# Fused retention attention and adapter mixture: short units stored in 64-row transfers, loads requested earlier, the fourth unit's scores moved, the last unit's slots in banks of their own

## The chip, the cores and the metric

The kernel runs on one core of one Trainium2 chip. The metric is device time in microseconds (us), the median over several executions. A core has a matrix engine (PE in the profile, with PEld for its weight loads), a vector engine (DVE), a scalar engine (ACT), a general engine (POOL) and a sync engine (SP); each runs its own instructions in order, and they meet through semaphores. DMA transfers are issued by SP, ACT or POOL and are carried by 16 DMA engines. Matrix results land in PSUM, which has eight banks that the kernel names by number.

## The reference

```python
scores = scale * q @ k^T                       # per batch (8) and head (8), 576 positions, 64 wide
Dmat   = where(i >= j, gamma_h ** (i - j), 0)  # decay mask
ret    = (scores * Dmat) @ v
x      = ret as rows (8 * 576 = 4608) x (8 heads * 64 = 512)
logits = x @ w_gate                            # 8 experts
top two experts per row, weights = softmax over the two
delta  = sum over the two of weight * ((x @ A[e]) @ B[e])     # rank 16
out    = x + delta                             # float32, 4608 x 512
```

## The kernel before, in words

The 576 positions of a sequence are four chunks of 128 and a last one of 64. A *unit* is one chunk of two batches; the last chunk takes four batches in one unit, with two batches on partitions 0 to 63 and two on 64 to 127 (a *short* unit). There are 18 units, t = 0 to 17; units 16 and 17 are short. A *quad* is one chunk of four batches, that is two full units or one short one, and `load(n, which)` fetches q, k or v of quad n: 1 MB for a full quad (4096 pieces of 256 B), and for a short one two transfers of 64 partitions. Each of q, k and v has three buffers, so quad n can be loaded when quad n-3 has been used up.

Per unit, with the function that issues each step: `scale` (POOL; DVE for unit 0) multiplies q and k by powers of gamma; `v_beside` (POOL) copies v next to the running state W; `pe_T` transposes k and q, `ev_Tk` and `ev_Tq` (ACT) evict them; `pe_S` makes the 64 x 64 scores, `ev_S` (DVE) masks them; `pe_U` makes the state updates, `ev_U` (DVE; ACT for the first chunk's half) adds them into W; `pe_RI` makes the attention output, transposed, and `ev_x` (ACT) evicts it as xT. Then comes the mixture: `pe_Z` computes the logits and all experts' z = x A into one PSUM bank (two *slots* s of 128 rows each), `route1`, `route_sig` and `route2` pick the two experts and mask z (DVE, two sigmoids on ACT), `pe_pzt` and `ev_pzt` transpose it, `pe_B` puts x back into row order in PSUM banks `po`, `pe_Y` adds z B to that, `ev_Y` (ACT) evicts the sum to `osb` (three buffers), and `store` sends it out, one transfer of 128 rows of 2 KB per slot. For the last unit `route_slot` routes one slot at a time, directly from PSUM.

The order is written out by hand: a preamble for units 0 to 4, then a loop over r = 3 to 16 in which round r does B and Y of unit r-2, Z of unit r-1, S and U of unit r+1, T of unit r+2, RI of unit r and the scaling of unit r+3; then an epilogue for the last three units (t = 17 there). Every PE operation goes through the helper `mm` (all PE work thus stands at L211 in the profile). `mm` keeps a count, and at set counts ("blocks") it takes one entry from the list `pending` and issues it with a dependence on the PE instruction that entered the block. Entries are loads (`later(n, which)`), the mixture's weights (`load_moe`: four 64 KB transfers in 64 B pieces and the small gate table) and stores. All of these but one early load go through SP's queue, in order; a DMA takes one of eight semaphores in turn.

The store of a short unit has a destination of its own form, since a slot holds 64 rows of each of two batches that are far apart in the output:

```python
b0 = QUAD * bp + s
dst = by_batch[b0 : b0 + 3 : 2, 128 * NFULL :, :]     # 2 x 64 x 512
```

The lines that the text names are these: L100 and L105 are the weight loads, L143 the full loads and L153 the short ones, L178 the copies of `v_beside`, L187 the scaling, L243 and L252 the evictions of kT and Q, L297 the masks, L337 and L339 the state updates, L371 xT, L395 zT, L419 to L450 the routing, L468 to L480 that of single slots, L511 `ev_Y`, L528 the stores.

Of the kernel before, what the change touches and what calls it, by code (L numbers as in the profile page):

```python
# [27 lines left out]
def kernel(  # L28
# [10 lines left out]
    nc = tc.nc  # L39
# [36 lines left out]


    BLOCK, BLOCK_FIRST = 253.6, 224

    def bank(n, shape, dtype=FP32, name="ps"):  # L80
        return pp.tile(shape, dtype, tag=f"bank{n}", name=name)
# [42 lines left out]
    def load(n, which, halves=(0, 2), eng=None, ins=None):  # L124

        if n >= len(quads):
            return
        eng = eng or nc.sync
        c, qd = quads[n]
        src, nat = {"q": (q, natq), "k": (k, natk), "v": (v, natv)}[which]  # L130
        lo, hi = halves
        if lo == 0:
            tl = iop.tile([128, QUAD * H, Dh], FP32, tag=which + "32", name=which + "32")
            if c < NFULL:
                for u in range(2):
                    nat[unit_of[(c, 2 * qd + u)]] = tl[:, 2 * H * u : 2 * H * u + 2 * H, :]
            else:
                nat[unit_of[(c, qd)]] = tl[:, 0 : 2 * H, :]
            load.tiles[(n, which)] = tl
        tl = load.tiles[(n, which)]  # L140
        if c < NFULL:
            b0 = QUAD * qd
            dma = eng.dma_start(  # L143
                out=tl[:, 2 * H * lo : 2 * H * hi, :],
                in_=src[b0 + 2 * lo : b0 + 2 * hi, :, 128 * c : 128 * c + 128, :].rearrange(
                    "b h j d -> j (b h) d"
                ),
            )
            behind(dma, ins)
        else:  # L150
            for g in range(2):
                b0 = QUAD * qd + 2 * g
                dma = eng.dma_start(  # L153
                    out=tl[half(g), 0 : 2 * H, :],
                    in_=src[b0 : b0 + 2, :, 128 * NFULL :, :].rearrange("b h j d -> j (b h) d"),
                )
                behind(dma, ins)
# [13 lines left out]
    def v_beside(t, eng_copy=nc.gpsimd.tensor_copy):  # L171

        if not 0 <= t < NU:
            return
        vn = natv[t].rearrange("p (s a o) d -> p o s a d", s=2, o=2)
        for g in range(2):
            for ho in range(2):
                eng_copy(out=W_of(t)[half(1 - ho), g, ho], in_=vn[half(g), ho])  # L178
# [27 lines left out]
    def behind(dma, ins):  # L206
        if ins is not None:
            tc.add_manual_dep(dma.ins, ins.ins.name, SYNC, reason="TensorE entered a block")
# [185 lines left out]
        sl = slice(slots[0], slots[-1] + 1)  # L394
        nc.scalar.copy(out=st[t]["zT"][:, sl], in_=st[t]["pzt"][:, sl])  # L395

    def pe_Z(t, s, b=3):
        if not 0 <= t < NU:
            return
        if s == 0:  # L400
            st[t]["pz"] = bank(b, [128, 2, ER + E], name="pz")
        for hp in range(HP):
            mm(
                st[t]["pz"][:, s, :],
                lhsT=st[t]["xT"][:, s, hp, :],
                rhs=AW[:, hp, 0 : ER + E],
                start=(hp == 0),
                stop=(hp == HP - 1),
                skip_group_check=True,
            )  # L410

    def route1(t):
        if not 0 <= t < NU:
            return
        pz = st[t]["pz"]
        lg = sm.tile([128, 2, E], FP32, tag="lg", name="lg")
        m8 = sm.tile([128, 2, E], FP32, tag="m8", name="m8")
        ns = sm.tile([128, 2], FP32, tag="ns", name="ns")
        nc.vector.tensor_copy(out=lg, in_=pz[:, :, ER : ER + E])  # L419
        for s in range(2):  # L420
            nc.vector.max(out=m8[:, s, :], in_=lg[:, s, :])
        nc.vector.scalar_tensor_tensor(
            out=ns, in0=m8[:, :, 0], scalar=-1.0, in1=m8[:, :, 1],
            op0=ALU.mult, op1=ALU.subtract,
        )
        st[t].update(lg=lg, m8=m8, ns=ns)

    def route_sig(t):
        if not 0 <= t < NU:
            return  # L430
        sg = sm.tile([128, 2, E], FP32, tag="sg", name="sg")
        for s in range(2):
            nc.scalar.activation(  # L433
                out=sg[:, s, :], in_=st[t]["lg"][:, s, :], func=AFT.Sigmoid,
                bias=st[t]["ns"][:, s : s + 1], scale=2.0,
            )
        st[t]["sg"] = sg
# [19 lines left out]

    def route_slot(t, s):

        pz = st[t]["pz"]  # L460
        if s == 0:
            for n in ("m8", "sg", "cm"):
                st[t][n] = sm.tile([128, 2, E], FP32, tag=n, name=n)
            st[t]["ns"] = sm.tile([128, 2], FP32, tag="ns", name="ns")
            st[t]["zc"] = mo.tile([128, 2, ER], FP16, tag="zc", name="zc")
        m8, ns, sg, cm, zc = (st[t][n] for n in ("m8", "ns", "sg", "cm", "zc"))
        lg = pz[:, s, ER : ER + E]
        nc.vector.max(out=m8[:, s, :], in_=lg)  # L468
        nc.vector.scalar_tensor_tensor(
            out=ns[:, s : s + 1], in0=m8[:, s, 0:1], scalar=-1.0, in1=m8[:, s, 1:2],  # L470
            op0=ALU.mult, op1=ALU.subtract,
        )
        nc.scalar.activation(
            out=sg[:, s, :], in_=lg, func=AFT.Sigmoid, bias=ns[:, s : s + 1], scale=2.0
        )
        nc.vector.scalar_tensor_tensor(
            out=cm[:, s, :], in0=lg, scalar=m8[:, s, 1:2], in1=sg[:, s, :],
            op0=ALU.is_ge, op1=ALU.mult,
        )
        nc.vector.tensor_tensor(  # L480
            out=zc[:, s].rearrange("p (e r) -> p e r", e=E),
            in0=pz[:, s, 0:ER].rearrange("p (e r) -> p e r", e=E),
            in1=cm[:, s].unsqueeze(2).broadcast_to((128, E, R)),
            op=ALU.mult,
        )
# [14 lines left out]
                    skip_group_check=True,  # L500
                )

    def ev_Y(t, slots=(0, 1), both=False):
        if not 0 <= t < NU:
            return
        if 0 in slots:
            st[t]["osb"] = mo.tile([128, 2, HP, 2, 64], FP32, tag="osb", name="osb", bufs=3)
        sl = slice(slots[0], slots[-1] + 1)
        for c in range(2):
            eng_copy = nc.vector.tensor_copy if both and c == 1 else nc.scalar.copy  # L510
            eng_copy(  # L511
                out=st[t]["osb"][:, sl, :, c, :].rearrange("p s a d -> p (s a) d"),
                in_=st[t]["po"][c][:, sl].rearrange("p s a d -> p (s a) d"),
            )

    def store(t, ins=None, slots=(0, 1)):
        if not 0 <= t < NU:
            return
        c_, bp = units[t]
        of = st[t]["osb"].rearrange("p s a o d -> p s (a o d)")  # L520
        by_batch = out.rearrange("(b n) d -> b n d", b=B)
        for s in slots:
            if c_ < NFULL:
                dst = by_batch[2 * bp + s, 128 * c_ : 128 * c_ + 128, :]
            else:
                b0 = QUAD * bp + s
                dst = by_batch[b0 : b0 + 3 : 2, 128 * NFULL :, :]
            behind(nc.sync.dma_start(out=dst, in_=of[:, s, :]), ins)  # L528


    def later(n, which):
        if n < len(quads):
            pending.append(lambda ins: load(n, which, ins=ins))
# [10 lines left out]
    load(1, "k")  # L544
    load(1, "q")
    load(1, "v")
    pending.append(load_moe)
    for which in ("k", "q", "v"):
        later(2, which)
    for t in range(4):  # L550
        clear_state(t, DV)
    PO.memset(ident16, 0.0)
# [56 lines left out]
    ev_U(2, 0)  # L609
    ev_U(2, 1)  # L610
    for which in ("q", "k", "v"):
        later(3, which)
    pe_Z(0, 0, 1)
    pe_Z(0, 1)
    route1(0)
    route_sig(0)
    route2(0)
    scale(5, "k", PO)
    scale(5, "q", PO)
    v_beside(4)  # L620
    for which in ("q", "k", "v"):
        later(4, which)
    pe_S(3, (6, 7))
    ev_S(3)
    pe_U(3, (2, 3))
    ev_U(3, 0)
    ev_U(3, 1)
    pe_B(0)
    pe_T(4, "k", (0, 2))
    ev_Tk(4)  # L630
    pe_pzt(0, 1)
    ev_pzt(0)
    pe_Z(1, 0, 6)
    pe_Z(1, 1)
    route1(1)
    pe_Y(0)
    ev_Y(0)
    route_sig(1)
    route2(1)
    pe_T(4, "q", (1, 7))  # L640
    ev_Tq(4, 0)
    ev_Tq(4, 1)
    pe_RI(2, (0, 2))
    ev_x(2)
# [51 lines left out]
    pe_Z(t - 1, 1)  # L696
    route1(t - 1)
    pe_Y(t - 2)
    ev_Y(t - 2)
    route_sig(t - 1)  # L700
    route2(t - 1)
    while pending:
        pending.pop(0)(None)
    store(t - 2)
    pe_Z(t, 0, 6)
    pe_Z(t, 1)
    route_slot(t, 0)
    route_slot(t, 1)
    pe_B(t - 1, (1, 7))
    pe_pzt(t - 1, 3)  # L710
    ev_pzt(t - 1)
    pe_B(t, (0, 2))
    pe_Y(t - 1)
    ev_Y(t - 1, both=True)
    store(t - 1)
    for s in range(2):
        pe_pzt(t, 4, (s,))
        ev_pzt(t, (s,))
    for s in range(2):
        pe_Y(t, (s,))  # L720
        ev_Y(t, (s,), both=True)
        store(t, slots=(s,))
    return


# [28 lines left out]
```

## Time and profile before

| | us |
|---|---|
| median of three runs | 213.53 (212.51 to 214.16) |
| profiled execution, whole | 215.45 |
| its span, first to last instruction | 213.5 |
| PE busy | 163.6 (77%) |
| DVE, ACT, POOL busy | 133.8, 119.1, 111.9 |
| first and last PE instruction | 7.01, 189.93 |
| last eviction of the output (DVE) | ends at 190.37 |

Times in the text are us from the start of the span. The granted clock of PE over the whole span is 0.937 of full speed. HBM was read for 28.98 MB and written for 9.44 MB.

### The profile page before, as it was taken

The page shows a single profiled execution, that of the slowest core. Times are in us where ns is not written, and L with a number is a line of the kernel's source. Part 1 is how long each engine was busy: PE and PEld are TensorE (multiplying, and loading weights), DVE is VectorE, ACT ScalarE, POOL GpSimd, SP SyncE. Part 2 cuts the span into 40 slices and gives each one's busy share as a digit, 9 for nine tenths or more (in the row PEclk, how much of TensorE's full clock was granted, in tenths as well). Part 3 has the DMA queues.
Part 4 walks back from the last instruction along what each step waited for, and adds up shares of the span by engine and source line. Part 5 has one row for each costly group of instructions (what it writes and reads, how often), then busy time and mean ns, then how long its engine had stood idle before and what let it go on. Part 6 is the DMA issues. An engine that isn't in the chain of part 4 may idle for free.

```text
span 213.5 us, 10240 instructions
## 1 busy us (share of the span) xinstructions
PE 163.6 (77%) x4588; PEld 148.9 (70%) x4588; DVE 133.8 (63%) x273; ACT 119.1 (56%) x246; POOL 111.9 (52%) x144
## 2 busy tenths in 40 slices
PE   0597967899798979988899898999898999920000
PEld 0496857789688979877788887888897999810000
DVE  6761744855968778697979686786969763430000
ACT  2486792589484567756565747666574837340000
POOL 1078983495799993995499189665009600000000
PEclk9999996999999999999999999999999999975555
DMA  7999966889898866957875884647445622201110
GB/s 170 260 209 281 296 82 190 240 250 291 226 263 232 300 200 202 305 163 195 245 276 162 250 234 169 155 93 251 102 112 149 242 101 101 101 11 46 51 51 38
DMA packets 56851, 38.93 MB, mean 182 GB/s; under 512 B 30441, under 2 KB 52201, under 8 KB 56809
## 3 DMA queue, kind: packets, MB, share of 16 engines
q1 hardware_dynamic: 54600, 37.64, 62.0%
q8 instruction: 36, 0.59, 1.1%
q10 hardware_dynamic: 2064, 0.52, 1.1%
q0 software_dynamic: 144, 0.13, 0.4%
q14 instruction: 7, 0.05, 0.1%
HBM read 28.98 MB, written 9.44 MB: 180 GB/s over the span
## 4 chain that ended last, share of the span: by engine, by line
PE 40%; POOL 16%; DMA 15%; DVE 8%; issue 5%; ACT 2%; SPq 2%; POOLq 0%; ACTq 0%
PE px L211 9%; PE pz L211 8%; DMA q<-in_q_dram 8%; DMA k<-in_k_dram 7%; POOL q L187 7%; PE ps_s L211 7%; POOL k L187 5%; POOL W L178 5%; PE po L211 4%; PE pu L211 4%; PE pt_k L211 4%; PE pt_q L211 4%; DVE Q L297 2%; DVE W L339 2%; DVE cm L446 2%
## 5 line engine op out<-in xcount | busy, mean ns | idle before, releaser
L297 DVE TENSOR_TENSOR Q<-ps_s,pack 64x512 f32<-64x512 f32 x72 | 49.6, 689 | 33.7 <-PE ps_s L211 32.6
L187 POOL TENSOR_TENSOR k<-k,pack 128x512 f32<-128x512 f32 x34 | 34.7, 1042 | 48.2 <-DMA k<-in_k_dram 35.0
L252 ACT COPY Q<-pt_q 64x512 f32<-64x512 f32 x72 | 41.8, 581 | 8.4 <-PE pt_q L211 7.6
L178 POOL COPY W<-v 64x512 f32<-64x512 f32 x68 | 41.5, 611 | 4.6 <-DMA v<-in_v_dram 1.4
L211 PE MATMUL pz<-AW,xT 128*128 128x136 f32 x288 | 39.1, 289 | 4.0 <-DMA AW<-in_moe_w_gate_dram 2.8
L339 DVE TENSOR_TENSOR W<-pu,W 64x512 f32<-64x512 f32 x56 | 38.4, 686 | 4.8 <-PE pu L211 3.8
L211 PE MATMUL px<-Q,W 128*64 128x64 f32 x1152 | 38.7, 225 | 1.4 <-DVE W L339 0.6
L211 PEld LDWEIGHTS pz<-AW,xT 128*128 128x128 f32 x288 | 36.1, 196 | 4.4 <-ACT W L337 2.9
L211 PEld LDWEIGHTS px<-Q,W 128*64 128x64 f32 x1152 | 35.8, 139 | 3.4 <-issue 0.9
L187 POOL TENSOR_TENSOR q<-q,pack 128x512 f32<-128x512 f32 x34 | 34.7, 1042 | 2.0 <-DMA q<-in_q_dram 2.0
L371 ACT COPY xT<-px 128x512 f32<-128x512 f32 x36 | 20.7, 585 | 13.7 <-PE px L211 13.4
L243 ACT COPY kT<-pt_k 128x512 f32<-128x512 f32 x34 | 18.3, 589 | 17.3 <-PE pt_k L211 17.3
L511 ACT COPY osb<-po 128x512 f32<-128x512 f32 (+1 forms) x35 | 18.5, 577 | 15.1 <-PE po L211 11.6
L211 PE MATMUL ps_s<-Q,kT 64*64 64x64 f32 x1152 | 23.2, 227 | 2.9 <-ACT Q L252 1.2
L211 PEld LDWEIGHTS ps_s<-Q,kT 64*64 64x64 f32 x1152 | 20.0, 139 | 4.8 <-ACT Q L252 2.7
L211 PE MATMUL pt_q<-pack,q 64*128 64x64 f32 x288 | 14.4, 232 | 8.3 <-DVE q L187 7.0
L211 PE MATMUL pu<-v,k 64*64 64x64 f32 x1024 | 20.0, 227 | 0.7 <-issue 0.7
L211 PEld LDWEIGHTS pu<-v,k 64*64 64x64 f32 x1024 | 17.9, 140 | 3.4 <-issue 3.4
L211 PE MATMUL pt_k<-pack,k 64*128 64x64 f32 x288 | 14.4, 238 | 6.6 <-POOL k L187 2.8
L211 PEld LDWEIGHTS pt_q<-pack,q 64*128 64x128 f32 x288 | 11.8, 144 | 9.5 <-DVE q L187 7.0
L446 DVE SCALAR_TENSOR_TENSOR cm<-lg,m,sg 128x8 f32<-128x8 f32 x34 | 16.0, 504 | 3.1 <-ACT sg L433 2.7
L211 PEld LDWEIGHTS pt_k<-pack,k 64*128 64x128 f32 x288 | 11.9, 147 | 8.3 <-POOL k L187 4.3
(34 smaller groups left out, 106.6 us busy)
## 6 DMA issues: line engine op xcount, KB each, us to landing
out_dram<-osb SPq DMA_DIRECT2D x36, 256.0 KB, 3.1
k<-in_k_dram SPq DMA_DIRECT2D x2, 512.0 KB, 5.9
v<-in_v_dram SPq DMA_DIRECT2D x2, 512.0 KB, 7.0
q<-in_q_dram SPq DMA_DIRECT2D x4, 256.0 KB, 4.2
k<-in_k_dram SPq DMA_DIRECT2D x4, 256.0 KB, 4.0
v<-in_v_dram SPq DMA_DIRECT2D x4, 256.0 KB
q<-in_q_dram ACTq DMA_DIRECT2D x1, 512.0 KB
q<-in_q_dram SPq DMA_DIRECT2D x1, 512.0 KB
```

The source lines that it names most:

```text
L178: eng_copy(out=W_of(t)[half(1 - ho), g, ho], in_=vn[half(g), ho])
L187: eng.tensor_tensor(out=x[:, s], in0=x[:, s], in1=tab[:, c, :].unsqueeze(2).broadcast_to((128, H, Dh)), op=ALU.mult,)
L211: ins = nc.tensor.matmul(out_, is_transpose=is_transpose, **kw)
L243: eng_copy(out=kT[:, g], in_=st[t]["ptk"][g])
L252: eng_copy(out=st[t]["Q"][half(ho), g, ho], in_=st[t]["ptq"][g][half(ho)])
L297: nc.vector.tensor_tensor(out=st[t]["Q"][half(1 - ho), :, ho, s, :, :], in0=st[t]["ps"][ho][half(s)], in1=tri[half(s), :].unsqueeze(1).uns ...
L339: nc.vector.tensor_tensor(out=f(dst[half(ho), dg, ho]), in0=f(st[t]["pu"][g][half(ho)]), in1=f(W[t][half(ho), g, ho]), op=ALU.add,)
L371: nc.scalar.copy(out=xT[:, s].rearrange("p a i -> p (a i)"), in_=st[t]["px"][s].rearrange("p a g i -> p (a g i)"),)
L446: nc.vector.scalar_tensor_tensor(out=cm[:, s, :], in0=lg[:, s, :], scalar=m8[:, s, 1:2], in1=sg[:, s, :], op0=ALU.is_ge, op1=ALU.mult,)
L511: eng_copy(out=st[t]["osb"][:, sl, :, c, :].rearrange("p s a d -> p (s a) d"), in_=st[t]["po"][c][:, sl].rearrange("p s a d -> p (s a) d"),)
```

## The change

There are four edits; a fifth, `PIECE`, cuts loads into transfers of at most four batches, which is what a full quad's load already was, so every load keeps its size.

1. A short unit's slot is stored in two transfers of 64 rows, one per batch (`half(g)` is a half of the partitions). The second transfer of the very last slot is issued by ACT.
2. The loads of quad 2 (the third) are no longer entries of `pending`. They are issued in the preamble at once, k ahead of the mixture's weights, q and v behind them. `pending` begins with quad 3, and quad 4 is appended where quad 3 was. The list is therefore shorter, and every later load and the first stores come off it two blocks earlier on PE's count: quad 5's q, for example, in RI of unit 4 instead of U of unit 6.
3. In the preamble S and U of unit 3 stand ahead of Z of unit 0 and its routing; Z of unit 1 stands ahead of unit 0's transposes of z, and the q transposes of unit 4 ahead of Y of unit 0, in banks 3 and 7.
4. In the epilogue the two slots of unit 17 have their logits in banks 6 and 0, and their routing is split: slot 0 is routed ahead of the z transposes of unit 16, slot 1 behind. The sigmoids of unit 16 stand between the two evictions of unit 15. B of unit 17 is issued whole, slot 0's z transposes go ahead of Y of unit 16.

The core of the diff:

```diff
-        by_batch = out.rearrange("(b n) d -> b n d", b=B)
         for s in slots:
             if c_ < NFULL:
-                dst = by_batch[2 * bp + s, 128 * c_ : 128 * c_ + 128, :]
-            else:
-                b0 = QUAD * bp + s
-                dst = by_batch[b0 : b0 + 3 : 2, 128 * NFULL :, :]
-            behind(nc.sync.dma_start(out=dst, in_=of[:, s, :]), ins)
+                n0 = S * (2 * bp + s) + 128 * c_
+                behind(nc.sync.dma_start(out=out[n0 : n0 + 128, :], in_=of[:, s, :]), ins)
+                continue
+            for g in range(2):
+                n0 = S * (QUAD * bp + 2 * g + s) + 128 * NFULL
+                eng = last if last and g == 1 else nc.sync
+                behind(eng.dma_start(out=out[n0 : n0 + 64, :], in_=of[half(g), s, :]), ins)
...
-    pending.append(load_moe)
-    for which in ("k", "q", "v"):
-        later(2, which)
+    load(2, "k")
+    load_moe()
+    load(2, "q")
+    load(2, "v")
+    for which in ("q", "k", "v"):
+        later(3, which)
...
     for which in ("q", "k", "v"):
-        later(3, which)
-    pe_Z(0, 0, 1)
-    pe_Z(0, 1)
-    route1(0)
-    route_sig(0)
-    route2(0)
+        later(4, which)
     scale(5, "k", PO)
-    scale(5, "q", PO)
-    v_beside(4)
-    for which in ("q", "k", "v"):
-        later(4, which)
     pe_S(3, (6, 7))
     ev_S(3)
     pe_U(3, (2, 3))
     ev_U(3, 0)
+    pe_Z(0, 0, 1)
+    pe_Z(0, 1)
     ev_U(3, 1)
+    route1(0)
+    route_sig(0)
+    route2(0)
     pe_B(0)
     pe_T(4, "k", (0, 2))
     ev_Tk(4)
+    pe_Z(1, 0, 6)
+    pe_Z(1, 1)
     pe_pzt(0, 1)
     ev_pzt(0)
-    pe_Z(1, 0, 6)
-    pe_Z(1, 1)
+    scale(5, "q", PO)
+    v_beside(4)
+    pe_T(4, "q", (3, 7))
+    ev_Tq(4, 0)
+    pe_Y(0)
     route1(1)
-    pe_Y(0)
     ev_Y(0)
...
-    ev_Y(t - 2)
+    ev_Y(t - 2, cs=(0,))
     route_sig(t - 1)
+    ev_Y(t - 2, cs=(1,))
     route2(t - 1)
...
-    pe_Z(t, 0, 6)
-    pe_Z(t, 1)
+    pe_Z(t, 0, 6, alone=True)
+    pe_Z(t, 1, 0, alone=True)
     route_slot(t, 0)
-    route_slot(t, 1)
     pe_B(t - 1, (1, 7))
     pe_pzt(t - 1, 3)
     ev_pzt(t - 1)
-    pe_B(t, (0, 2))
+    route_slot(t, 1)
+    pe_B(t)
+    pe_pzt(t, 2, (0,))
+    ev_pzt(t, (0,))
     pe_Y(t - 1)
     ev_Y(t - 1, both=True)
     store(t - 1)
-    for s in range(2):
-        pe_pzt(t, 4, (s,))
-        ev_pzt(t, (s,))
-    for s in range(2):
-        pe_Y(t, (s,))
-        ev_Y(t, (s,), both=True)
-        store(t, slots=(s,))
+    pe_pzt(t, 2, (1,))
+    ev_pzt(t, (1,))
+    pe_Y(t, (0,))
+    ev_Y(t, (0,), both=True)
+    store(t, slots=(0,))
+    pe_Y(t, (1,))
+    ev_Y(t, (1,), both=True)
+    store(t, slots=(1,), last=AC)
```

More of the change, by code (lines that the diff above doesn't have):

```diff
@@ L78 @@
     BLOCK, BLOCK_FIRST = 253.6, 224
+    PIECE = 4
     def bank(n, shape, dtype=FP32, name="ps"):
@@ L141, in load @@
         if c < NFULL:
[L142 to L149, printed above, removed]
+            for b in range(2 * lo, 2 * hi, PIECE):
+                b0, nb = QUAD * qd + b, min(PIECE, 2 * hi - b)
+                dma = eng.dma_start(
+                    out=tl[:, H * b : H * (b + nb), :],
+                    in_=src[b0 : b0 + nb, :, 128 * c : 128 * c + 128, :].rearrange(
+                        "b h j d -> j (b h) d"
+                    ),
+                )
+                behind(dma, ins)
         else:
@@ L395, in ev_pzt, with pe_Z @@
         nc.scalar.copy(out=st[t]["zT"][:, sl], in_=st[t]["pzt"][:, sl])
-    def pe_Z(t, s, b=3):
+    def pe_Z(t, s, b=3, alone=False):
         if not 0 <= t < NU:
             return
-        if s == 0:
+        if s == 0 or alone:
             st[t]["pz"] = bank(b, [128, 2, ER + E], name="pz")
+            st[t][f"pz{s}"] = st[t]["pz"]
         for hp in range(HP):
@@ L458, in route_slot @@
     def route_slot(t, s):
-        pz = st[t]["pz"]
+        pz = st[t][f"pz{s}"]
         if s == 0:
@@ L501, in pe_Y, with ev_Y @@
                 )
-    def ev_Y(t, slots=(0, 1), both=False):
+    def ev_Y(t, slots=(0, 1), both=False, cs=(0, 1)):
         if not 0 <= t < NU:
             return
-        if 0 in slots:
+        if 0 in slots and 0 in cs:
             st[t]["osb"] = mo.tile([128, 2, HP, 2, 64], FP32, tag="osb", name="osb", bufs=3)
         sl = slice(slots[0], slots[-1] + 1)
-        for c in range(2):
+        for c in cs:
             eng_copy = nc.vector.tensor_copy if both and c == 1 else nc.scalar.copy
@@ L514, in ev_Y, with store @@
             )
-    def store(t, ins=None, slots=(0, 1)):
+    def store(t, ins=None, slots=(0, 1), last=None):
         if not 0 <= t < NU:
@@ L639 @@
     route2(1)
-    pe_T(4, "q", (1, 7))
-    ev_Tq(4, 0)
     ev_Tq(4, 1)
```

## The prediction

> **What bounds the kernel now.** I read the slices of the page first, then SP's waits and the timeline at the end, then PE's idle stretches by time, and for each of them what DVE, POOL and SP did there.
>
> ```profile
> PE   0597967899798979988899898999898999920000
> PEclk9999996999999999999999999999999999975555
> DMA  7999966889898866957875884647445622201110
> GB/s 170 260 209 281 296 82 190 240 250 291 226 263 232 300 200 202 305 163 195 245 276 162 250 234 169 155 93 251 102 112 149 242 101 101 101 11 46 51 51 38
> ```
>
> A slice is 213.5 / 40 = 5.3 us. PE is near full up to slice 35 and then nothing runs for four slices while the DMA engines move about 50 GB/s at a busy share of one tenth. The kernel has two parts: 7 to 190 us, which PE's order sets, and a tail of 23 us (190.37 to 213.5) in which only stores move. The next views say what these are: SP's waits, its timeline, and busy time by stretch (the last two columns are the DMA share and GB/s).
>
> ```profile
> SPq L749 <- DMA out_dram<-osb: 13.6, 1, 13.6
> 188.86 9.77 SPq L528 DMA_DIRECT2D out_dram<-osb  x4
> 189.95 0.42 DVE L511 COPY osb<-po 128x256 f32<-128x256 f32 x1 [0.36 <-PE po L211]
> 134.00:137.00 3.00, 2.96 (x92) 2.73 (x86) 2.82 (x6) 1.70 (x4) 2.75 (x5) 1.00 0.79 180
> 185.00:187.00 2.00, 1.68 (x36) 1.27 (x34) 1.32 (x7) 0.39 (x2) 0.00 (x0) 1.00 0.68 262
> 196.00:212.00 16.00, 0.00 (x0) 0.00 (x0) 0.00 (x0) 0.00 (x0) 0.00 (x0) 0.50 0.13 51
> ```
>
> The four L528 transfers from 188.86 are the short units' slots, 256 KB each. From 196 to 212 they hold the DMA engines at a share of 0.13, which is 2 of 16, at 51 GB/s or 25.5 GB/s for each of the two; 4 x 262 KB / 51 GB/s = 20.5 us, the tail. The 128-row store in 185 to 187 shows 0.68 and 262 GB/s although it fills only part of the stretch. The two forms differ in the destination, two pieces of 64 rows against 128 rows in a row. And 134 to 137 holds the short loads (L153), which are transfers of 64 partitions: 0.79. So it is not the 64 partitions that confine a transfer to two engines.
>
> In the front part PE idles twice in a way that bears on the change: at the first logits (16 matmuls pz, 3.48 us against 2.07 later, after 2.78 us of waiting for the weights), and ahead of transposes of k:
>
> ```profile
> PE pz L211 <- DMA AW<-in_moe_w_gate_dram: 2.8, 1, 2.8
> 36.81 1.16 PE L211 MATMUL ps_s<-Q,kT 64*64 64x64 f32 x64
> 38.83 0.71 PE L211 MATMUL po<-pack,xT 64*128 64x64 f32 x16
> 75.13 2.04 POOL L187 TENSOR_TENSOR k<-k,pack 128x512 f32<-128x512 f32 x2
> 75.51 1.68 DVE L446 SCALAR_TENSOR_TENSOR cm<-lg,m,sg 128x8 f32<-128x8 f32 x2
> 77.22 0.42 DVE L450 TENSOR_TENSOR zc<-pz,cm 128x256 f16<-128x256 f32 x1
> 77.75 0.72 PE L211 MATMUL pt_k<-pack,k 64*128 64x64 f32 x16 [1.14 <-POOL k L187]
> ```
>
> The last line blames POOL, but the k in question was scaled at 68.36. The transposes go into bank 3, where z stands until zc (77.22 to 77.64) has read it, and zc was late because the two cm ran 1.68 us where they take 0.42 when POOL is not scaling. The waits of POOL for k loads (35.0 us in all, the longest row of waits) are thus mostly slack: T of units 8 and 10 (1.14 and 1.54 us) waits for zc with k long ready.
>
> **The change, part by part**, against the profiled span of 213.5. The whole of that execution took 215.45; the median of the runs is 213.53, by chance the span's own length, so I give the new span as the new median.
>
> *Stores and epilogue.* The routing of unit 16 no longer waits for unit 15's second eviction (0.59): its first cm starts at about 184.04 instead of 184.44, and slot 0's routing (185.24 to 186.56, five steps on DVE and ACT) ends at about 186.15. zT of unit 16, which stood behind slot 1's sigmoid on ACT (187.04 to 187.40), can go when its transposes are done, at 186.1 to 186.5. B of unit 17 (0.71) hides that. Y of unit 16 follows at 186.9 instead of 187.46, its evictions end at 188.25 instead of 188.80. Then slot 1's transposes, Y, and evictions with the same durations as before put the last eviction at 189.45 instead of 190.37. Moving slot 1's logits to bank 0 costs nothing: that bank was evicted by 180.8. It adds eight issues where there were four. SP issues seven; an ordinary store's issue is 0.43 us (median of 36) plus 0.06 between two. From 188.3 the seventh starts at 188.3 + 6 x 0.49 = 191.2; landing takes 2.2 us (2.1 to 2.3 for the stores of 184) and gives 193.4; SP then needs the 1.1 us that it needed from 212.4 to 213.5. The eighth, on ACT, starts at 189.5 and lands ahead of the seventh; ACT has nothing behind it. End: 194.5, a gain of **19.0**. Bytes do not set it: 1.05 MB at 262 GB/s are 4.0 us, from 188.3 to 192.3. Bounds: in most runs of four stores one issue takes 1.4 us instead of 0.43, once or twice here, so 17 to 19 in all; with the minimum issue of 0.33 it is 19.6.
>
> [...]
>
> *Weights behind k of quad 2.* SP's queue is backed up there. Its 1 MB loads start at 14.70, 18.44 and 22.1: 3.7 us for each. Putting one ahead of the weights moves them from 33.4 to about 37.1, while k of quad 2 is ready about 7 us sooner (38.8 before). Against this, S and U of unit 3 now go first. They need the scores' bank 7 (mask of unit 2 ends at 32.45) and end at 34.8 at full clock, 36.8 at half. Z of unit 0 then runs from 37.1 to 39.2, and B of unit 0, which started at 38.83, starts at 39.2: a loss of 0.4. Behind it T of k4 no longer waits (39.54 to 41.39 becomes 0.7, a gain of 1.1); T of q4 still hangs on q, which has the same bytes ahead of it as before. RI of unit 2 (44.97) comes out between 43.8 and 46.4: gain 1.2 to loss 1.4. I take **0**: PE's wait for the weights is only split, 1.8 us ahead of S and 2.3 us ahead of Z. Queued behind Z on PE is everything from B of unit 0 on.
>
> *Loads two blocks earlier.* Two blocks are one round, some 9.7 us (transposes of k from 57.47 to 164.84 in 11 rounds). Buffers are free by then: quad 4 takes quad 1's, whose last reader, U of unit 3, is through. On SP the waits for PE shrink (17.4 us at L143 behind pu), and stores behind these loads are asked for a round earlier too, so nothing piles up. What PE gains is less. Tied to late loads or late POOL work are 0.51 us (q of unit 6, 58.44) and 0.83 us (unit 17, 164.0, when POOL's last work falls on zc): **1.3**. The upper bound is all of PE's idle time ahead of transposes from 39 to 165: 0.39 + 0.28 + 0.23 + 1.02 + 0.51 + 1.14 + 0.30 + 1.54 + 0.89 + 0.26 + 0.83 = 7.4. The lower bound is a loss of 2: POOL's scaling moves by a round against DVE's cm, and each round in which they newly meet costs 0.9 to 1.5. I take a value near the low end because POOL's scaling keeps its place within a round and moves by a whole one, so cm will meet it about as often.
>
> *Sum:* 213.5 - 19.0 - 0 - 1.3 = **193.2**.
>
> **The rivals.** (1) *The early loads free PE.* If POOL finishes ahead of the routing in most rounds, the 7.4 us above go nearly whole: 213.5 - 19.0 - 6 = 188.5. For it: POOL waits 35.0 us for k; against it: k was ready when PE waited. (2) *The weights become the wait.* If they land later than 37.1, or Z of unit 0 runs at half clock (3.48), and the cm meet POOL more often: 1.4 + 2 lost, 196.6. For it: the half clock at 33 to 36; against it: S and U now keep PE busy there. (3) *The stores do not spread*: 64-row pieces still on two engines, 20.5 us as before: 213.5 - 0.9 - 1.3 = 211.3, within 1% or just beyond. Against it: the short loads' 0.79. (4) *Slower than before*: if each 64-row transfer goes to one engine and all to the same, eight of 131 KB at 25.5 GB/s take 41 us from 188.3, and the end is 231. It decides from the point where fewer than two engines work at a time. The same row stands against it.
>
> **How the numbers follow.** Forecast 0.60, rival 1 0.20, rival 2 0.15, rival 3 0.02, rival 4 0.03. The range reaches from 188.0, so that it takes in the middle of rival 1, to 196.8, which takes in most of rival 2 and the slow issues of stores. A measurement of this kernel tells about 1% from no change. Faster by over 1%: 0.95; within 1%: 0.02; slower: 0.03.
>
> **What would show it.** The DMA share after 189 us should be five tenths or more for some 3 us, and SP's last wait for `out_dram<-osb` about 2 us. The first pz should start between 36 and 38 at a PE idle time named AW. POOL's waits for k should fall below half of 35 us while the idle time ahead of pt_k stays above 3 us. If the DMA share in the tail stays at one tenth, the main term is wrong; if PE's last instruction is before 185, the small one for the loads is.

## The result and the profile after

The changed kernel took 199.06 us (196.71 to 199.6, four runs), the kernel before 213.26 us beside it (four runs): ratio 0.931, interval 0.923 to 0.940. It is faster, as forecast, but 5.9 us slower than the 193.2 of the forecast and outside the range. The profiled execution took 196.71 us in all with a span of 194.6; some 2 us (1.8 to 2.2) lie around the span in every execution here, before and after. Ratios take fast executions alone, those within 1.5% of the fastest of the same kernel; medians take all.

The slices of the changed kernel (PE, the granted clock, the DMA share, GB/s):

```profile
PE   0598884988899898989999988899689999999950
PEclk9999998799999999999999999999999999999995
DMA  7999997799899896988798967547254514223046
GB/s 170 284 231 266 274 287 118 179 269 262 230 305 261 247 296 182 304 278 242 229 315 270 277 190 262 118 111 217 109 115 108 115 56 167 111 111 111 24 144 159
```

PE is now busy up to slice 38 of 40 (a slice is 4.9 us), and the last slices move 144 and 159 GB/s where they moved some 50. SP's last wait, the timeline at the end, and two stretches of the tail (last two columns: DMA share, GB/s):

```profile
SPq L758 <- DMA out_dram<-osb: 1.7, 3, 0.6
187.25 4.53 SPq L532 DMA_DIRECT2D out_dram<-osb  x7
187.88 0.42 DVE L514 COPY osb<-po 128x256 f32<-128x256 f32 x1 [0.36 <-PE po L213]
188.39 0.56 ACTq L532 DMA_DIRECT2D out_dram<-osb  x1
189.00:190.00 1.00, 0.00 (x0) 0.00 (x0) 0.00 (x0) 0.00 (x0) 0.00 (x0) 0.96 0.87 201
190.00:193.00 3.00, 0.00 (x0) 0.00 (x0) 0.00 (x0) 0.00 (x0) 0.00 (x0) 0.50 0.89 240
```

The DMA share of the tail went from 0.13 to 0.88, and from the last eviction (188.30) to the end of the span it is 6.3 us where it was 23.1. But the seven issues on SP run 4.53 us, 0.65 each with the gap, not the 0.49 that the forecast took. Ahead of the tail:

```profile
32.29 0.94 PE L213 MATMUL pu<-v,k 64*64 64x64 f32 x41 [2.51 <-issue]
36.95 2.12 PE L213 MATMUL pz<-AW,xT 128*128 128x136 f32 x16
39.00 0.71 PE L213 MATMUL po<-pack,xT 64*128 64x64 f32 x16
POOL k L189 <- DMA k<-in_k_dram: 28.0, 5, 13.8
PE pu L213 <- issue: 3.9, 4, 2.5
PE pzt L213 <- issue: 1.8, 1, 1.8
PE px L213 <- issue: 1.5, 3, 0.5
```

The first pz starts where the forecast put it (36.95). New is a kind of idle time that the forecast never looked at: PE stands still with no semaphore to wait for ("issue"), once for 2.51 us. Summed over PE's idle stretches longer than 0.15 us, this kind was 4.0 us before and is 11.4 after, while stretches that a semaphore ended fell from 22.2 to 12.4. (Without the 1.8 us ahead of pzt it is 9.6, the figure that the expectations below have. A semaphore that this pzt needs comes 0.5 us into the stretch; the 1.3 us left after it have none.)

**What PE waits for there.** The table of DMA queues has a queue called instruction, with the same 36 packets in both kernels:

```profile
q8 instruction: 36, 0.59, 1.2%
```

I take these 36 packets of 16 KB for PE's instructions: the trace has 9269 rows of PE, its weight loads and its sequencer, 257 to a packet. Nearly all of the nameless idle stretches (25 of 26, before and after) stand 127 matmuls apart, or a multiple of it, to within one; with the weight loads that is 254 rows, about one packet. They end some 2.5 us after one of these packets starts (2.2 to 2.6 in 23 of the 26, the others 2.9, 3.1 and 4.2). The helper's `BLOCK = 253.6` is this size, and an entry of `pending` is let go some 20 matmuls behind these places (matmul 619 by the helper's count, and the stretch that ends at 32.29 stands at 599). On this reading PE has then just gone over from one packet to the next.

**The end is rigid.** Cut each trace at the end of the last px matmul and at the last eviction. In all 17 traces the pieces behind the cuts depend only on edits 1 and 4 (and by 0.1 us on who issues the last stores):

| | last px to last eviction | last eviction to end |
|---|---|---|
| before | 10.26 | 23.1 |
| changed, and every version with edits 1 and 4 on SP and ACT (12 traces) | 9.01 to 9.02 | 6.33 to 6.35 |
| edit 1 alone; the old end of group 3 below | 10.26 | 6.36 and 6.37 |
| last stores on three queues | 9.02 | 6.23 |
| all but edit 1 | 9.02 | 23.55 |

So edits 1 and 4 are worth 16.75 + 1.24 = 18.0 us in every execution. The median fell by only 14.2. The rest of the kernel, up to the last px, thus became 3.8 us *longer*: 213.26 - 2.0 - 23.1 - 10.26 = 177.9 before, 199.06 - 2.0 - 6.34 - 9.02 = 181.7 after. I call this the front part; in the experiments it is worked out in the same way from the medians of runs. (The two profiled executions hide it: before's was 2.2 us above its median, the other 2.35 below.)

### The profile page after: what moved, and what is told of

Same layout as the page of the kernel before. It is cut to its first block, busy times and chain, and to the rows that moved or that the text cites. A ratio compares the mean times of both kernels' runs of the same rounds, so it can differ in the third digit from the quotient of the medians.

```text
span 194.6 us, 10239 instructions
## 1 busy us (share of the span) xinstructions
PE 163.8 (84%) x4588; PEld 149.1 (77%) x4588; DVE 129.8 (67%) x273; ACT 120.0 (62%) x246; POOL 112.0 (58%) x144
## 4 chain that ended last, share of the span: by engine, by line
PE 68%; DVE 10%; issue 9%; ACT 5%; POOL 4%; DMA 1%; DVEq 0%; POOLq 0%; ACTq 0%
PE px L213 15%; PE pz L213 14%; PE ps_s L213 10%; PE pu L213 8%; PE po L213 8%; PE pt_k L213 5%; PE pt_q L213 5%; ACT Q L254 3%; DVE Q L299 2%; DVE W L341 2%; PE pzt L213 2%; DVE cm L449 2%; POOL q L189 2%; POOL W L180 1%; DVE W L171 1%
## 5 line engine op out<-in xcount | busy, mean ns | idle before, releaser
L213 PE MATMUL px<-Q,W 128*64 128x64 f32 x1152 | 39.3, 225 | 1.8 <-issue 1.5
L213 PEld LDWEIGHTS px<-Q,W 128*64 128x64 f32 x1152 | 36.3, 139 | 4.0 <-issue 2.0
L213 PE MATMUL pz<-AW,xT 128*128 128x136 f32 x288 | 37.8, 283 | 0.6 <-issue 0.6
L213 PEld LDWEIGHTS pz<-AW,xT 128*128 128x128 f32 x288 | 34.7, 190 | 0.3 <-issue 0.2
L213 PE MATMUL ps_s<-Q,kT 64*64 64x64 f32 x1152 | 24.3, 232 | 3.7 <-ACT Q L254 1.4
L213 PEld LDWEIGHTS ps_s<-Q,kT 64*64 64x64 f32 x1152 | 21.1, 144 | 6.1 <-ACT Q L254 3.0
L245 ACT COPY kT<-pt_k 128x512 f32<-128x512 f32 x34 | 18.3, 590 | 12.1 <-PE pt_k L213 12.0
L514 ACT COPY osb<-po 128x512 f32<-128x512 f32 (+1 forms) x35 | 18.6, 577 | 10.6 <-PE po L213 10.5
L213 PE MATMUL pu<-v,k 64*64 64x64 f32 x1024 | 21.3, 230 | 3.9 <-issue 3.9
L213 PEld LDWEIGHTS pu<-v,k 64*64 64x64 f32 x1024 | 18.8, 143 | 7.0 <-issue 7.0
L213 PE MATMUL pt_q<-pack,q 64*128 64x64 f32 x288 | 13.9, 231 | 7.5 <-DVE q L189 6.6
L449 DVE SCALAR_TENSOR_TENSOR cm<-lg,m,sg 128x8 f32<-128x8 f32 x34 | 13.0, 415 | 5.0 <-ACT sg L436 4.6
```

The costliest lines, as they stand in the source:

```text
L213: ins = nc.tensor.matmul(out_, is_transpose=is_transpose, **kw)
L245: eng_copy(out=kT[:, g], in_=st[t]["ptk"][g])
L449: nc.vector.scalar_tensor_tensor(out=cm[:, s, :], in0=lg[:, s, :], scalar=m8[:, s, 1:2], in1=sg[:, s, :], op0=ALU.is_ge, op1=ALU.mult,)
L514: eng_copy(out=st[t]["osb"][:, sl, :, c, :].rearrange("p s a d -> p (s a) d"), in_=st[t]["po"][c][:, sl].rearrange("p s a d -> p (s a) d"),)
```

## The experiments

Six executions each, four of the version with all but edit 1. Kernels of one group ran beside the kernel before on the same chip. "Front" is the front part against that of before in the same group; "issue" is PE's idle time without a semaphore, in the profiled execution (it was 4.0 before and 11.4 after the change).

| group, run | median us | ratio to before, interval | front | issue |
|---|---|---|---|---|
| 1 the change again | 201.47 | 0.947 (0.940 to 0.954) | +6.1 | 14.7 |
| 1 edit 1 alone | 198.76 | 0.925 (0.914 to 0.936) | +2.1 | 4.1 |
| 1 all but edit 1 | 218.31 | none | +5.7 | 12.1 |
| 1 all but edit 2 | 198.18 | 0.921 (0.911 to 0.932) | +2.8 | 5.6 |
| 2 all but edit 2, again | 196.05 | 0.913 (0.909 to 0.917) | -0.6 | 5.8 |
| 2 the same, gates 112 instructions sooner | 204.94 | 0.949 (0.942 to 0.956) | +8.3 | 17.9 |
| 2 first loads early, later ones as before | 197.22 | 0.918 (0.914 to 0.923) | +0.5 | 5.2 |
| 2 all but edit 2, last stores on three queues | 196.43 | 0.915 (0.910 to 0.919) | -0.1 | 4.1 |
| 3 the change again | 198.47 | 0.923 (0.911 to 0.934) | +1.4 | 10.4 |
| 3 two empty entries | 197.86 | 0.921 (0.912 to 0.931) | +0.8 | 6.7 |
| 3 four empty entries | 196.62 | 0.920 (0.911 to 0.929) | -0.4 | 5.9 |
| 3 four empty entries, old end | 198.88 | 0.921 (0.905 to 0.937) | +0.6 | 5.5 |
| 4 the change again | 200.88 | 0.925 (0.919 to 0.931) | +5.3 | 10.6 |
| 4 four empty entries | 197.17 | 0.915 (0.910 to 0.921) | +1.6 | 7.3 |
| 4 one empty entry | 197.77 | none | +2.2 | 8.4 |

**The parts of the change.** The change once more, as the standard of the first group:

> The changed kernel once more, unaltered, for its spread and a second trace. Theory F (the loads asked for at once stand ahead of PE's own instruction fetches on the DMA engines): idle time of PE that no semaphore explains is 8 us or more again (9.6 in the first trace, 4.0 before the change), with one wait of 2 us or more in U of unit 2 near 30 us, and each such wait ends about 2 us after a 16 KB packet of the instruction queue starts. Rival G (that idle time is chance, and the early loads cost nothing): it falls towards 4 us and the spans move with it. Time 197 to 200 either way.

The idle time came again, 14.7 us, and with it theory F's late packets; the one wait near 30 us did not. The longest is 3.37 us, near 119 us, and ends 2.5 us after a packet starts.

Edit 1 alone, on the kernel before, all stores on SP:

```diff
-                dst = by_batch[b0 : b0 + 3 : 2, 128 * NFULL :, :]
-            behind(nc.sync.dma_start(out=dst, in_=of[:, s, :]), ins)
+            for g in range(2):
+                n0 = S * (QUAD * bp + 2 * g + s) + 128 * NFULL
+                behind(nc.sync.dma_start(out=out[n0 : n0 + 64, :], in_=of[half(g), s, :]), ins)
```

> The kernel before with edit 1 alone (64-row stores, all on SP). The tail falls from 23 us to about 6: 213.3 - 16.5 = 196.8. If F holds, the other edits then lose time or win none: this kernel is as fast as the changed one (196 to 198). If the early loads pay as forecast, this one is slower than the changed kernel by 2 us or more.

Everything but edit 1, that is the reverse of this diff on the changed kernel, with all stores on SP:

> The changed kernel with the old store of short slots (2 x 64 rows, on SP). If the stores are the whole gain: 211 to 214. The DMA share after the last eviction is 0.13 again, at 51 GB/s. If the other edits gain 1.3 us as forecast, 212; if they lose, 214 or more.

And everything but edit 2:

```diff
-    load(2, "k")
-    load_moe()
-    load(2, "q")
-    load(2, "v")
-    for which in ("q", "k", "v"):
-        later(3, which)
+    pending.append(load_moe)
+    for which in ("k", "q", "v"):
+        later(2, which)
...
     ev_U(2, 1)
     for which in ("q", "k", "v"):
+        later(3, which)
+    for which in ("q", "k", "v"):
         later(4, which)
```

> The changed kernel with edit 2 undone: weights and quad 2 come off the list of pending loads again, and quads 3 and 4 behind them. F: the wait of 2.5 us in U of unit 2 is gone, idle PE time without a semaphore falls from 9.6 to some 4 us, and the kernel gains 1 to 4 us over the changed one in the same call (195 to 198). Forecast (loads earlier gain 1.3): it is 1 to 2 us slower than the changed one. G: the same within 0.5 us.

Edit 1 by itself gives 14.6 us, more than the whole change in this group (11.9). Without it nothing is gained (one of four executions took 212.2 us, the others 218 to 220), and the tail is the old one. The stretch of it in the version with all but edit 1:

```profile
200.00:216.00 16.00, 0.00 (x0) 0.00 (x0) 0.00 (x0) 0.00 (x0) 0.00 (x0) 0.50 0.13 51
```

Share 0.13 and 51 GB/s as before, so it is the form of the short stores that spreads them, and no other edit. Taking edit 2 out of the change makes it 3.3 us faster, with intervals that don't touch: here the early loads cost time. (Edit 1 alone touches only the last two units' stores, and yet its front is 2.1 us longer than that of before: so much do medians of one group scatter.)

**How loads reach PE.** SP's timeline over about one cycle of loads shows a difference; first all but edit 2 (group 2), then the change (group 3; the second number is how long the issues took):

```profile
78.06 0.70 SPq L145 DMA_DIRECT2D k<-in_k_dram  x1
82.40 0.70 SPq L145 DMA_DIRECT2D v<-in_v_dram  x1
86.67 2.44 SPq L527 DMA_DIRECT2D out_dram<-osb  x4
91.19 0.71 SPq L145 DMA_DIRECT2D q<-in_q_dram  x1
```

```profile
62.63 6.03 SPq L527 DMA_DIRECT2D out_dram<-osb  x4
68.88 0.72 SPq L145 DMA_DIRECT2D q<-in_q_dram  x1
70.05 5.18 SPq L145 DMA_DIRECT2D k<-in_k_dram  x1
75.69 3.22 SPq L145 DMA_DIRECT2D v<-in_v_dram  x1
79.03 6.60 SPq L527 DMA_DIRECT2D out_dram<-osb  x4
```

With the loads at their old places a load's issue takes 0.70 us, and SP waits for PE between them (93 us in all). In the change SP comes late to most entries, its waits for PE fall to 46 to 61 us, each of these rows but q's takes 3.2 to 6.6 us, which I read as the load ahead still being worked off, and loads and stores follow with hardly a gap. My theory F, which no view shows directly: PE's instruction packets are carried by the same 16 engines, and one that comes behind such a load is late by what is left of it. If that is so, moving the same loads by less than a block must cost more than edit 2 does. The standard for this, again:

> The changed kernel with the third quad's and all later loads put back behind block entries (edit 2 undone), once more, as the standard for the three beside it. It stood at 0.9213 [0.911, 0.9317] of the kernel before. All theories: 0.915 to 0.93, 196 to 199 us; TensorE idle time that the waits name 'issue' 4 to 7 us.

The same kernel with one number changed (this moves the stores among the entries too):

```diff
-    BLOCK, BLOCK_FIRST = 253.6, 224
+    BLOCK, BLOCK_FIRST = 253.6, 112
```

> As the standard, with one number changed: the counter at which a pending load is let go stands 112 TensorE instructions (about 2.3 us) sooner, so a load is asked for ahead of TensorE's own 16 KB instruction packet and not behind it. Order and number of all transfers are the same and every load comes sooner. Theory F (the early loads cost time because instruction packets queue behind loads on the same 16 DMA engines): 'issue' idle up by 4 to 10 us, time up by 2 to 6 us against the standard. Rival G (the early loads cost time in another way, such as slots or stores that come late, and packet order is nothing): 'issue' idle within 2 us of the standard, time the same or up to 1.5 us less, since loads come sooner.

It is 8.9 us slower although every load is asked for 2.3 us sooner: F, by more than its 2 to 6, and G falls. PE's waits without a semaphore in this version, and one of them in PE's timeline:

```profile
PE pt_k L213 <- issue: 4.6, 2, 2.5
PE px L213 <- issue: 4.0, 5, 1.9
PE po L213 <- issue: 3.8, 2, 2.0
PE pu L213 <- issue: 2.5, 3, 1.5
PE ps_s L213 <- issue: 2.5, 3, 1.0
```

```profile
88.15 0.48 PEld L213 LDWEIGHTS pt_k<-pack,k 64*128 64x128 f32 x12
90.91 0.34 PE L213 MATMUL pt_k<-pack,k 64*128 64x64 f32 x5 [2.17 <-issue]
```

PE stops in the middle of a group of transposes, at matmul 1993, and goes on 2.4 us after a packet starts at 88.47. The v load asked for at 82.99 had its first engine through at 88.48 and its last at 89.01. So the packet began just when the engines came free of this load. Issue time rose by 12.1 us and the front part by 8.9; semaphore waits did not change (17.5 and 18.1). That the packet stood in line behind the load is read from these times; no run takes the packets away.

**Which loads.** The third quad and the weights early as in the change, all later loads at the old entries:

```diff
+    for _ in range(4):
+        pending.append(lambda ins: None)
```

> Only half of edit 2: the third quad and the weights are requested at once in the preamble, as in the changed kernel, while the loads from the fourth quad on are let go at the same block entries as in the standard (four empty entries stand in for the ones taken out). Theory F1 (the backlog is made by asking for the fourth and later quads about a round sooner): time as the standard within 1.5 us, 'issue' idle 4 to 7 us, SP again waits for TensorE more than 40 us in all. Rival F2 (the burst in the preamble by itself makes the backlog on SP's queue): time 2 to 4 us above the standard, 'issue' idle 8 to 13 us.

197.22 against 196.05 with overlapping intervals, and issue time 5.2: the burst in the preamble is not what costs (F1). Group 3 was to show a dose:

> The changed kernel unaltered, as the standard for the three beside it: no empty entries ahead of the fourth quad's loads. It stood at 0.947 [0.9402, 0.9539] and at 0.9311 [0.9228, 0.9395] of the kernel before. 198 to 202 us, 'issue' idle of TensorE 9 to 13 us.

> The changed kernel with two empty entries ahead of the fourth quad's loads, so that each later load is let go two block entries after where the changed kernel lets it go and two ahead of where the old order would. Theory F1 (cost by how far SP's queue runs ahead of the block entries): time and 'issue' idle between the standard and the version with four, 199 us and 7 to 9 us. Rival (a threshold: any entry at all between them lets SP wait for each entry again): as with four empty entries, within 1 us.

> The same with four empty entries (the run before, repeated beside its neighbours; it stood at 0.9183 [0.9136, 0.9231]). Theory F1: 196 to 198 us, 2 to 4 us below the standard, 'issue' idle 5 to 6 us, SP waiting for TensorE about 90 us in all. Rival F2 (the preamble's burst costs most of the difference): within 1.5 us of the standard.

This was a poor experiment. The list runs empty before the fourth quad's loads are appended, so two empty entries and four give the same waits on every DMA. The two runs are one kernel twice, and their 1.2 us is the scatter. In this group the change is 0.6 and 1.9 us above them, inside the intervals. The third attempt, meant to have the loads one block ahead from the fifth quad on:

```diff
+    pending.append(lambda ins: None)
     for which in ("q", "k", "v"):
         later(4, which)
```

> The changed kernel unaltered (later loads two block entries ahead of the old places). Theory F (instruction packets behind loads): 'issue' idle of TensorE 8 to 13 us, 198 to 202 us. Rival N (edit 2 costs nothing on the whole, and the difference seen before is the scatter of runs): as the version with four empty entries within 1 us.

> Third quad and weights early, all later loads at the old block entries. Theory F: 5 to 6 us of 'issue' idle, 196 to 198 us. Rival N: as the changed kernel within 1 us.

> The changed kernel with one empty entry ahead of the fifth quad's loads: from there on every load stands one block entry ahead of its old place (in the changed kernel two), and the third and fourth quads' loads are as early as in the changed kernel. Theory F with the place in the block deciding (a load let go at any block entry stands behind the packet asked for there, as long as SP comes to it in time): 'issue' idle 5 to 8 us, within 1.5 us of the version with four empty entries. Rival A (cost by how far ahead a load is asked for): halfway, 'issue' idle 8 to 9 us.

This attempt missed its aim too. In the changed kernel the list runs empty once more, between the fifth quad's loads and the first stores, and the empty entry only fills that gap. It moves the fifth quad's three loads back by one block; from the first stores on, every load and store stands at the same entry as in the change. SP's queue agrees: the first four stores and the next three loads are issued in 5.91, 0.71, 5.61 and 3.23 us from 63.17 on, in the change (above) in 6.03, 0.72, 5.18 and 3.22 us from 62.63 on, and SP waits 39.7 us for PE, not 93. The version is the change in all but three loads, and yet its median is 3.1 us below that of the change beside it. Its issue time of 8.4 us lies in rival A's range and its median in theory F's, but neither is tested by it, and a difference of 3 us between two medians of one group is not by itself a price.

Taken together the runs still speak against N. The change is 3.7 us above the version with the old entries in group 4 (2.0 by the ratios, whose intervals overlap slightly). In the first result and in groups 1, 3 and 4 its medians (198.5 to 201.5) lie above the six of the versions with the old entries (196.1 to 198.2); the means are 200.0 and 197.2, or 199.5 with the one-entry version counted as the change. The price is some 2 to 3 us. The traces show where it lies. Issue time is 10.4 to 14.7 us in the four traces of the change (8.4 with one empty entry), 4.1 to 7.3 in the eight with the old entries. All idle time of PE up to the last px is 28.0 us on average in the four (23.4 to 32.4; 22.1 with one empty entry), 23.9 in the eight (22.2 to 25.7): in some executions shorter semaphore waits make up for the late packets, in most they don't.

Much of the scatter is something else, the granted clock. Up to the last px it is at half for none to four stretches of 3.4 us, whatever the version, and PE's time outside idle stretches goes with it: 155 us with none, 157 with two, 159 with four. Between the two traces of group 4 (four stretches in the change, one with the old entries) this makes 3.8 us.

**The tail.** Two rivals for the 6.3 us behind the last eviction, the chain of SP's issues or full DMA engines:

```diff
-                eng = last if last and g == 1 else nc.sync
+                eng = (last or second or nc.sync) if g == 1 else nc.sync
...
-    store(t - 1)
+    store(t - 1, second=PO)
...
-    store(t, slots=(0,))
+    store(t, slots=(0,), second=PO)
```

> As the standard, with the eight last 64-row stores spread over three queues: SP issues four in place of seven, GpSimd three, ScalarE one. Theory T (the tail after the last eviction is SP's chain of issues, 0.67 us each): the tail falls from about 5.3 us (last eviction to last landing) by three issues, 2.0 us; time 1.5 to 2.5 us below the standard. Rival U (the eight transfers, 1 MB, fill the DMA engines for those 5 us, and an issue takes 0.67 us only because the engines are full): below 0.7 us gained, and the issues on the three queues are as long together.

```profile
186.75 3.19 SPq L532 DMA_DIRECT2D out_dram<-osb  x4
187.28 1.66 POOL L532 DMA_DIRECT2D out_dram<-osb  x3 [19.13 <-DVE osb L514]
187.89 0.57 ACTq L532 DMA_DIRECT2D out_dram<-osb  x1
188.00:192.00 4.00, 0.00 (x0) 0.00 (x0) 0.00 (x0) 0.00 (x0) 0.94 (x2) 0.90 0.89 259
```

All eight are issued within 3.2 us instead of 4.5, and the end moves by 0.1 us (6.23 from the last eviction): U. The engines are at a share of 0.89 here and in the change, and the 1 MB takes 4 to 5 us in both (in the change its packets run from 188.47 to 193.20; here the rate is 2 GB/s in 192 to 193).

The old end (edit 4 undone), with the loads of the four empty entries:

```diff
-    pe_Z(t, 0, 6, alone=True)
-    pe_Z(t, 1, 0, alone=True)
+    pe_Z(t, 0, 6)
+    pe_Z(t, 1)
     route_slot(t, 0)
+    route_slot(t, 1)
...
-    store(t, slots=(1,), last=AC)
+    store(t, slots=(1,))
```

> As the one with four empty entries, but with the last stage as it was before the change (edit 4 undone; all eight last stores on SP). By the sum of the prediction: last eviction about 0.9 us later against the start of unit 15's B, and SP issues eight, so the end 1 to 1.6 us later. Rival E (the DMA engines are full for the last 5 us, so the end is the first of those stores plus 6.2 us, whoever issues them): the end moves only by what the first of the eight stores moves.

In its trace the last eviction comes 1.24 us later against the last px, and eight issues on SP in place of seven cost 0.03 us, so the end moves by 1.27 us, within the sum's 1 to 1.6. The first of the eight stores moves by 0.79 us only: E falls. The medians are 198.88 and 196.62 with wide intervals; the trace is what prices it.

## Why the prediction was wrong

| term | forecast | measured | miss |
|---|---|---|---|
| base: the profiled span for the median before | 213.5 | 213.26 | -0.2 |
| routing and evictions of the epilogue | -0.92 | -1.24 | -0.3 |
| last eviction to the end | -18.1 (23.13 to 5.05) | -16.75 | +1.3 |
| front part: weights 0, loads -1.3 | -1.3 | +3.8 | +5.1 |
| sum | 193.2 | 199.06 | +5.9 |

*Stores: the mechanism right, the size 1.3 us too large.* The step that was mis-sized is the tail behind the last eviction, 5.05 us in the sum and 6.34 measured. The forecast let SP issue at 0.49 us, a rate at which the eight stores would have moved their 1.05 MB in 3.9 us, at 267 GB/s. It had "bytes do not set it" from 262 GB/s, the rate in 185 to 187, where a 128-row store ran. The tail moved 201 to 240 GB/s at a share of 0.87 to 0.89, an issue took 0.65 us there, and spreading the issues bought 0.1 us. Rivals 3 and 4 fell with the share of 0.88. Rival 2 came nearest in time (196.6), but not by its mechanism: the first pz took 2.12 us, not the 3.48 of half clock.

The row at 196 held: one store into two pieces of 64 rows ran at a share of 0.13, two stores of one piece each at 0.88. Why the first form stays at 0.13 is not shown; no run tries a third.

*Weights behind k: right.* First pz at 36.95 (forecast 37.1), B of unit 0 at 39.00 (39.2), RI of unit 2 at 44.42 (between 43.8 and 46.4). The idle time named AW, which was to stand ahead of it, is missing in the profiled execution, where a late packet had delayed PE by 2.51 us already; in the change's second trace it is there:

```profile
PE pz L213 <- DMA AW<-in_moe_w_gate_dram: 2.4, 1, 2.4
```

*Loads two blocks earlier: the step that failed.* It is the sentence "so nothing piles up". Stores and loads did pile up on SP, where in group 3 the issue of a k load took 5.18 us and that of a v load 3.22 in place of 0.70. "Two blocks" was also short for the first of them: counted in the list, the fourth quad's loads come five blocks earlier and the fifth's three. And what was late next was no buffer and no semaphore but, by the evidence above, PE's instructions, a transfer that the forecast had not counted although the profile lists its queue. Its lower bound, a loss of 2 for POOL against cm, was of another mechanism. The gain was looked for in the right place: PE's idle time ahead of pt_k fell from 6.5 to 2.4 us in the profiled execution, below the 3 that the forecast named, as rival 1 had it, though POOL's waits for k only went from 35.0 to 28.0. But in the other three traces of the change it was 3.3 to 7.5 us, and semaphore waits were 18 us, no less than without the early loads (17 to 20). Against that stands issue time of 10.4 to 14.7 us, with the old entries 4.1 to 7.3. Some 3 of the 5.1 us of the miss (2 to 3 by all the runs) are thus put down to the early loads. The rest is the gain of 1.3 that isn't there, and 0.8 us on average in the versions with the old entries, which the scatter doesn't resolve. The sign "PE's last instruction before 185" did not come (187.84): as such it said nothing of a loss.

*A span is not a median.* Giving the new span as the new median dropped the 2.0 us around it; it came out nearly even only because the execution profiled before was 2.2 us above its median. With the median as base the same terms give the same sum, by luck.

What stays open: why the price of the early loads goes from 0.6 to 3.7 us between groups, whether it grows with how far ahead a load is asked for, which no run tests, and what edit 3 brings by itself (all but edit 2 stands 0.6 us below edit 1 alone, where edit 4 alone accounts for 1.24). The version with everything but edit 2 is faster than both kernels: 198.18 against 201.47 for the change in the first group, 196.05 in the second.

## What to carry to other kernels

Cut a trace where the work is rigid and price each piece against the medians: two profiled executions at opposite ends of their scatter had shown a gain of 0.8 us in the front part where the medians have a loss of 3.8. Before transfers are asked for earlier, look at what else the table of DMA queues lists, here the instruction queue, and at where PE stands still without a semaphore: loads asked for 112 instructions sooner (56 matmuls with their weight loads), ahead of these places instead of some 20 behind them, cost 8.9 us here. When a list of pending work decides when a transfer is asked for, count its entries, the empty ones too, before a run is taken for a dose. For a store, read its DMA share in the profile: the destination in two pieces had 0.13 here, one piece per transfer 0.88, and at 0.89 two more queues moved the end by 0.1 us.

## What the runs showed of the hardware

- The queue "instruction" carried 36 packets of 16 KB, and PE's 9269 rows are 257 to a packet. PE stood still without a semaphore for 4 to 18 us of some 200, up to 3.4 us at a time; before and after the change 25 of 26 such stretches stood a multiple of 127 matmuls apart, and 23 ended 2.2 to 2.6 us after a packet's start. Asking for loads 2.3 us sooner cost 8.9 us.
- A store with a destination of two separate blocks of 64 rows ran at a DMA share of 0.13, as much as 2 of 16 engines, and 51 GB/s; two stores of 64 rows each at 0.88 and 201 to 240 GB/s.
- An issue of a load on SP took 0.70 us where SP waited 93 us in all for PE, and in the change, where it waited 46 to 61 us, 0.72 (q), 5.18 (k) and 3.22 us (v).
- The granted clock fell to half for none to four stretches of 3.4 us ahead of the tail, in executions of one and the same kernel too. By the 155 and 159 us above a stretch cost some 1 us, an estimate.
